# Contiguous DRAM layouts for u, its residual copy, w_mod, the raw parameters and the result, and an earlier place for the tables of the second DFTs

## The chip, the core and the metric

The kernel runs on one core of a Trainium2 chip. The core has five engines that run side by side and wait for each other by semaphores: TensorE (PE, matmuls and their weight loads), VectorE (DVE), ScalarE (ACT), GpSimd (POOL) and SyncE (SP, which here only issues DMAs). Sixteen DMA engines move data between DRAM and the core's memory; DMAs are issued from the queues of SP, POOL and ACT, in program order on each. The metric is the device time of one execution in microseconds (us), as the median of several runs.

## What is computed

One residual block with adaptive layer norm. A state-space convolution (S4) of length 2048 runs over 512 channels, then a spatial-shift mixer and a channel MLP follow. Cut to what matters here:

```python
mod = (_silu(c) @ w_mod).reshape(c.shape[0], 6, 1, -1)
sa, ca, ga, sb, cb, gb = (mod[:, 0], mod[:, 1], mod[:, 2], mod[:, 3], mod[:, 4], mod[:, 5])
h = _layernorm(x, axis=-1) * (1 + ca) + sa
x = x + ga * _A_ref(h, ...)          # A_u is x; S4: K = einsum(C, exp(dt*A*l), dt*B).real,
...                                  # y = irfft(rfft(pad(K)) * rfft(pad(h)))[:L] + h * Dskip
h = _layernorm(x, axis=-1) * (1 + cb) + sb
x = x + gb * _B_ref(h, ...)          # gelu(LN(h) @ w1), shifts by +1, -1, +2, -2, @ w2,
...                                  # then gelu(LN @ w3) @ w4
```

All arrays are float32. `A_u` is (1, 2048, 512) and `w_mod` is (512, 3072).

## The kernel before

The convolution is done as a DFT of length 4096, factored into 64 x 64. The order of all work is written out by hand (`tc.manual_schedule()`): each engine runs its instructions in the order of the program text, and the framework adds the semaphores. The stages are:

- *Preparation* (`body`, up to `pr.close()`): small inputs and the raw parameters `raw` (ar, ai, cr, br, ci, bi) are loaded from SP, and the constants PA, CE, C0, PB, C1 from POOL. `load_mod(0..2)` loads three of the six blocks of `w_mod` into parts of the tile KX, and `load_u(0)`, `load_u(1)` load the first half of u into the two buffers of the pool `up` (tiles named `xu`).
- *Generation*: a loop over 32 chunks `k` (`turns`, `products`, `burst`) makes the convolution kernel K and the first DFT of it in KX. Beside it, by the lists `side[k]`, u is normalised (`u_stats`, `u_norm`) and its first DFT (`u_dft`) is stored to the DRAM scratch VU, 128 KB at a time from SP, out of the tiles `vs`. The other blocks of `w_mod` come by `load_mod(3..5)` into the one buffer of the pool `wml`, and the rest of u by `load_u(2)`, `load_u(3)`. POOL copies w2, w3 and w4 from DRAM to a DRAM scratch here.
- `k_first(0..7)`: matmuls with FK out of KX into the tiles VK, evicted by ACT and DVE.
- *Spectral steps*: a loop `n` over 16 steps (jh, kc). `spectrum_k` makes the second DFT of K with the table T2 (in two tiles named `xu`) and a flipped copy T3 of it that POOL makes (`flip`). `multiply` multiplies with the spectrum of u on DVE (tiles ma, mb, then zc). `back` applies the inverse DFT's first half (Gm), ACT copies the result to the tile z (a pool of two buffers) and POOL issues its store to the scratch ZT, in two DMAs of 64 partitions each. `spectrum_u(n + 1)` makes the second DFT of u out of VU with the table TU, and `load_vu(n + 3)` loads VU for a later step into one of seven buffers `ld`. The residual x, the same array as u, is loaded into X2, which is the memory of KX, by `load_x` in the steps 3, 4, 6 and 8. Between the steps also lie the loads of w1, FI and w2 and the first blocks of the inverse.
- *Inverse, mixer, channel MLP*: the inverse reads ZT, adds to X2, and `chan_out` writes each finished block of 128 rows to the result.

The sequences of 32 partitions: u is taken apart as 4 groups of 32 partitions (`bp`), two of them with the rows of time in reverse order, hence four DMAs per `load_u` and `load_x`, and four per block of the result.

PE's code is a straight line of 14,390 instructions.

Of the kernel before, what the change touches and what calls it, by code (L numbers as in the profile page):

```python
# [7 lines left out]
F32 = mybir.dt.float32  # L8
# [13 lines left out]
UB = (1, 2, 0, 3)  # L22
# [61 lines left out]
def layouts(inp):  # L84
    a = lambda n: np.asarray(inp[n])
    perm = lambda x: np.ascontiguousarray(x.reshape(2, 2, 2, 16, 4, -1).transpose(1, 3, 0, 2, 4, 5).reshape(512, -1))
    m = {"u": a("A_u")[0], "wm": a("w_mod"), "c": np.ascontiguousarray(a("c").reshape(4, 128).T),
         "ld": np.ascontiguousarray(perm(a("A_log_dt")).reshape(4, 128).T),
         "dk": np.ascontiguousarray(a("A_Dskip").reshape(2, 2, 2, 64).transpose(0, 2, 1, 3).reshape(4, 128)),
         "w1": a("B_w1"), "w2": a("B_w2"), "w3": a("B_w3"), "w4": a("B_w4")}  # L90
    for k, n in (("ar", "A_A_re"), ("ai", "A_A_im"), ("br", "A_B_re"), ("bi", "A_B_im"),
                 ("cr", "A_C_re"), ("ci", "A_C_im")):
        m[k] = perm(a(n))
    m.update(shape_constants())
    return m


def dram(t, off, ap):
    return bass.AP(tensor=t.tensor, offset=t.offset + off, ap=ap)


def body(ctx, tc, A):
    nc = tc.nc
    V, S, P, T, Y = nc.vector, nc.scalar, nc.gpsimd, nc.tensor, nc.sync
# [59 lines left out]
    a12 = ExitStack()  # L164
# [2 lines left out]
    Kq = KX.rearrange("p (g h c) -> p h g c", g=64, h=2)  # L167
    X2 = KX.rearrange("p (b d) -> p b d", b=16)
    up = a12.enter_context(pool("up", bufs=2))
    FK = pa12.tile([128, 128], F32, name="FK")  # L170
    sp1 = pa12.tile([128, 1], F32, name="sp1")
    V.memset(sp1, 0.0)
# [27 lines left out]
    wmt = {}  # L200

    def load_mod(n):
        wmt[n] = KX[:, n * 2048:n * 2048 + 2048].rearrange("p (a b) -> p a b", a=4) if n < 3 else \
            wml.tile([128, 4, 512], F32, name="wm")
        Y.dma_start(wmt[n], dram(A["wm"], MODS[n] * 512, [[3072, 128], [128 * 3072, 4], [1, 512]]))


    def mod_parts(n):
# [16 lines left out]

    def load_u(g):
        x = ut[g] = up.tile([128, 4, 512], F32, name="xu")
        for n, bp in enumerate(UB):
            Y.dma_start(x[n * 32:(n + 1) * 32],
                        dram(A["u"], (bp * 16 + g * 4) * 512, [[64 * 512, 32], [1, 2048]]) if bp > 1 else  # L230
                        dram(A["u"], (bp * 16 + 15 - g * 4) * 512, [[64 * 512, 32], [-512, 4], [1, 512]]))

    pe = a1.enter_context(pool("pe", bufs=2))
    PE, KP = {}, {}
# [42 lines left out]
    with tc.manual_schedule():  # L277
        Y.dma_start(ld[:, :4], A["ld"])
        Y.dma_start(cT, A["c"])
        for k in raw:  # L280
            Y.dma_start(raw[k], A[k].rearrange("(t p) n -> p t n", p=128))
        gate = pp.tile([128, 4], F32, name="gate")
        P.tensor_copy(gate[:, 0:1], raw["ai"][:, 0, 0:1])
        for k, t in (("PA", PA.rearrange("p a b c -> p (a b c)")), ("CE", CE), ("C0", C0),
# [113 lines left out]
        V.tensor_tensor(as4(wn), as4(wn), by(dt), op=OP.mult)  # L398
    pr.close()

    wml = a1.enter_context(pool("wml", bufs=1, reuse_waits="tile"))
    wk = a1.enter_context(pool("wk", bufs=2, reuse_waits="tile"))
    wk1 = a1.enter_context(pool("wk1", bufs=1, reuse_waits="tile"))
    uv = a1.enter_context(pool("uv", bufs=2, reuse_waits="tile"))
# [112 lines left out]
    for i in range(16):  # L517
# [5 lines left out]
        if i % 4 == 3 and i < 8:  # L523
            side[at(i) + 2].append(lambda i=i: load_u(i // 4 + 2))

    def add_skip(h, g0, g1):
        V.tensor_add(Kq[:, h, g0:g1, 31], DS[:, h * 64 + g0:h * 64 + g1], Kq[:, h, g0:g1, 31])

    later = []
    with tc.manual_schedule():  # L530
        turns(0, 0)
        turns(0, 1)
        wps = psu.tile([128, 512], F32, name="pu")
        for i in range(4):
            T.transpose(wps[:, i * 128:i * 128 + 128], wn[:, i * 128:i * 128 + 128], ident)
        act(WN, wps)
        ms = [mod_sum(n) for n in range(2)]
        turns(1, 0)
        for f in ms:
            f()  # L540
        turns(1, 1)
        later.append(mod_parts(2))
        late = [lambda: later.append(mod_sum(2))]
        for k in range(33):
            now, later = later, []
            for f in now:
                f()
            if k + 2 < 32:
                turns(k + 2, 0)
                turns(k + 2, 1)  # L550
            while late:
                late.pop()()
            if k < 32:
                fresh = k % 4 == 1 and k < 28
                if fresh:
                    exps(k // 4 + 1, 0, 2)
                e = products(k)
                if k == 31:
                    warm(8)
                    add_skip(0, 0, 64)  # L560
                    add_skip(1, 0, 56)
                burst(k, *e)
                if k == 31:
                    warm(4)
                if fresh:
                    KP[1] = psk.tile([128, 8, 64], F32, name="kp")
                    fill(3)
                    for u in range(2, 5):
                        exps(k // 4 + 1, u, u + 1)
                        if u < 4:  # L570
# [12 lines left out]
        T2 = [up.tile([128, 16, 128], F32, name="xu") for i in range(2)]  # L583
        load_t2 = lambda i: Y.dma_start(T2[i], A["T2"].rearrange("p (a b) -> p a b", a=32)[:, i * 16:i * 16 + 16])
        load_t2(0)
    a1.close()


    a2 = ExitStack()
    v0x = ExitStack()  # L590
    c2 = a2.enter_context(pool("c2"))
    TU = c2.tile([128, 32, 64], F32, name="TU")
    Gm = c2.tile([128, 2, 64], F32, name="Gm")
    FI = c2.tile([128, 32, 2, 32], F32, name="FI")
    VK = [v0x.enter_context(pool("v0", side="right")).tile([128, 64, 2, 64], F32, name="VK0"),
# [111 lines left out]
        q.dma_start(zis[jh, k][:, a:a + n], dram(ZT[jh], (k * 4 + a) * 32768, [[256, 128], [32768, n], [1, 256]]))  # L707

    def load_x(g):
        for bp in range(4):  # L710
            Y.dma_start(X2[bp * 32:(bp + 1) * 32, g * 4:g * 4 + 4],
                        dram(A["u"], (bp * 16 + g * 4) * 512, [[64 * 512, 32], [512, 4], [1, 512]]))

    def inv_half(jh, g, i, pl, name):
        p = pl.tile([128, 2, 256], F32, name=name)
# [242 lines left out]
    def chan_out(g, acc, i, qs):  # L958
        b = 2 * g + i
        o = c2p.tile([128, 512], F32, name="gf")  # L960
        V.tensor_mul(o, acc[i], mods[5])
        V.tensor_add(X2[:, b], X2[:, b], o)
        for bp in range(4):
            qs[bp % len(qs)].dma_start(dram(A["out"], (bp * 16 + b) * 512, [[64 * 512, 32], [1, 512]]),
                                       X2[bp * 32:(bp + 1) * 32, b])

    def chan(g, hl):
        t = g + 3 if 0 < g < 4 else None
# [114 lines left out]

    steps = [(jh, kc) for jh in range(2) for kc in range(8)]
    with tc.manual_schedule():
        tu = A["TU"].rearrange("p (a b) -> p a b", a=32)
        load_vu(*steps[0])
        Y.dma_start(TU[:, :16], tu[:, :16])
        flip(0)
        Y.dma_start(Gm, A["G"].rearrange("p (a b) -> p a b", a=2))  # L1090
        for r in range(8):
# [7 lines left out]
        for n, st in enumerate(steps):  # L1099
            p = spectrum_k(*st)  # L1100
            multiply(*st, us, p)
            if n == 7:
                v0x.close()
                pw2 = ctx.enter_context(pool("pw2", side="right", reuse_waits="tile"))
                pw1 = ctx.enter_context(pool("pw1", side="right", reuse_waits="tile"))
                W2h, W2l, ldw2 = weights(pw2, WD["w2"], 512, 512, "w2", 4)
                W1h, W1l, ldw1 = weights(pw1, A["w1"], 512, 512, "w1", 4)
            if n > 0:
                back(*steps[n - 1])
            if n == 15:  # L1110
# [185 lines left out]
```

## Time and profile before

| what | value |
|---|---|
| runs | 698.31, 698.88, 703.15 us; median 698.88 |
| the profiled execution | 701.46 us, its span 699.7 us |
| busy share of the span | PE 91%, weight loads 72%, DVE 71%, ACT 47%, POOL 18% |
| mean granted TensorE clock | 0.986 |
| data moved | 86.43 MB, mean 124 GB/s |
| preparation | about 0 to 35 us |
| generation | about 35 to 208 us |
| k_first | about 208 to 223 us |
| spectral steps | about 223 to 315 us |
| inverse, mixer, channel MLP | about 315 to 700 us |

The DMAs that the change touches, by their sizes in the profile: raw parameters 6 x 256 KB, w_mod 6 x 1024 KB, u 16 x 256 KB, x 16 x 256 KB, T2 2 x 1024 KB, TU 2 x 512 KB, result 64 x 64 KB.

How to read the lines of the profile: an instruction is named by its engine, its line in the program ("L666"), its operation and its tiles (output <- inputs). "Idle before, releaser" is the time that the engine stood still just ahead of an instruction and what ended that; "issue" stands for idle time for which the profile shows no releaser. A DMA named with SPq, POOLq or ACTq is its issue on that queue, not its transfer. The DMA share is the mean busy share of the 16 DMA engines; it can read a little over 1. The chain of waits follows the work that ended last back from the end, each time to what released it.

### The profile page before, as it was taken

How to read it: one execution, taken by the hardware profiler on the slowest of the kernel's cores; microseconds unless marked ns; L12 is line 12 of the kernel's file. 1: busy time of each engine (PE TensorE's matmuls, PEld its weight loads, DVE VectorE, ACT ScalarE, POOL GpSimd, SP SyncE). 2: the span in 40 equal slices, each digit the busy share in tenths (PEclk: the TensorE clock that was granted, in tenths of full speed). 3: DMA queues.
4: the chain of work that ended last, by engine and by line, in shares of the span. 5: the costliest groups of instructions: out<-in, count | busy, mean ns of one | idle time of the engine just before them, and what ended most of it. 6: DMA issues, size and time to landing. Idle time of an engine off the chain costs nothing.

```text
span 699.7 us, 16980 instructions
## 1 busy us (share of the span) xinstructions
PE 639.1 (91%) x7195; PEld 507.1 (72%) x7195; DVE 497.8 (71%) x795; ACT 331.9 (47%) x505; POOL 125.3 (18%) x236
## 2 busy tenths in 40 slices
PE   1899999999999588885998999999999999999996
PEld 0456655656569456653778889999899989889895
DVE  7899999999987567995986967566554536363522
ACT  3978998889856344650444633124131222213120
POOL 4011122022103335431661101002010000000000
PEclk9999999999999889998999999999999999999999
DMA  8903274745539999987268111020110201011011
GB/s 269 297 9 89 77 214 116 197 104 176 147 88 349 231 277 327 292 288 243 90 192 303 40 31 31 15 72 20 46 31 16 76 1 42 20 34 27 1 31 30
DMA packets 57731, 86.43 MB, mean 124 GB/s; under 512 B 5812, under 2 KB 43704, under 8 KB 56216
## 3 DMA queue, kind: packets, MB, share of 16 engines
q1 hardware_dynamic: 53320, 66.74, 34.0%
q0 software_dynamic: 3440, 17.57, 7.4%
q10 hardware_dynamic: 896, 1.05, 0.6%
q8 instruction: 56, 0.92, 0.5%
q14 instruction: 19, 0.16, 0.1%
HBM read 59.12 MB, written 32.90 MB: 132 GB/s over the span
## 4 chain that ended last, share of the span: by engine, by line
PE 69%; DVE 17%; issue 4%; DMA 4%; ACT 3%; POOL 1%; SPq 0%; ACTq 0%; DVEq 0%; POOLq 0%
PE pm L829 7%; PE pm L827 7%; PE pm L826 7%; PE pa L950 6%; PE pa L942 6%; PE pa L943 6%; PE xx L446 6%; PE pk L666 3%; PE kp L496 3%; PE pz L688 2%; DVE e L464 2%; DVE e L474 2%; PE pk L612 2%; PE ph L881 2%; PE ph L883 2%
## 5 line engine op out<-in xcount | busy, mean ns | idle before, releaser
L110 ACT ACTIVATE gh<-pm 128x512 fp32r<-128x512 f32 (+1 forms) x48 | 26.9, 561 | 200.6 <-PE pm L829 200.6
L826 PE MATMUL pm<-nh,w3h 128*128 128x256 f32 (+1 forms) x352 | 85.8, 279 | 2.1 <-ACT nh L110 2.1
L827 PE MATMUL pm<-nh,w3l 128*128 128x256 f32 (+1 forms) x352 | 85.7, 279 | 0.1
L934 DVE TENSOR_TENSOR gl<-gf,gh 128x512 fp32r<-128x512 f32 (+1 forms) x48 | 30.8, 643 | 68.3 <-ACT gf L110 68.3
L942 PE MATMUL pa<-w4h,gh 128*128 128x512 f32 (+1 forms) x176 | 69.6, 395 | 0.0
L943 PE MATMUL pa<-w4l,gh 128*128 128x512 f32 (+1 forms) x176 | 68.9, 392 | 0.0
L826 PEld LDWEIGHTS pm<-nh,w3h 128*128 128x128 f32 (+1 forms) x352 | 65.3, 185 | 3.8 <-ACT nh L110 2.3
L827 PEld LDWEIGHTS pm<-nh,w3l 128*128 128x128 f32 (+1 forms) x352 | 65.3, 185 | 2.2 <-DVE w3l L744 0.5
L753 POOL TENSOR_TENSOR rs<-mv,eps_t 128x1 f32<-128x1 f32 (+1 forms) x39 | 11.0, 283 | 281.8 <-DVE mv L759 264.7
L829 PE MATMUL pm<-nl,w3h 128*128 128x256 f32 (+1 forms) x352 | 54.8, 277 | 0.0
L950 PE MATMUL pa<-w4h,gl 128*128 128x512 f32 (+1 forms) x176 | 48.1, 390 | 0.8 <-DVE gl L934 0.8
L447 PE MATMUL xx<-MG,ON 64*128 64x512 f32 x160 | 47.1, 390 | 0.0
L446 PE MATMUL xx<-MG,ON 64*128 64x512 f32 x160 | 47.1, 389 | 0.0
L829 PEld LDWEIGHTS pm<-nl,w3h 128*128 128x128 f32 (+1 forms) x352 | 46.6, 185 | 0.2 <-DVE nl L799 0.2
L666 PE MATMUL pk<-VK,xu 64*64 64x128 f32 x768 | 36.8, 274 | 10.7 <-issue 10.7
L886 DVE TENSOR_TENSOR h<-h,ph 128x512 f32<-128x512 f32 x16 | 11.0, 687 | 45.1 <-PE ph L883 45.1
L666 PEld LDWEIGHTS pk<-VK,xu 64*64 64x64 f32 x768 | 32.7, 135 | 14.0 <-issue 13.2
L464 DVE SCALAR_TENSOR_TENSOR e<-tr,p 128x512 f32<-128x512 f32 x64 | 41.1, 682 | 0.4 <-ACT tr L110 0.4
L496 PEld LDWEIGHTS kp<-e,e 128*32 128x32 f32 x2048 | 30.1, 110 | 13.1 <-issue 7.5
L950 PEld LDWEIGHTS pa<-w4h,gl 128*128 128x128 f32 (+1 forms) x176 | 33.0, 188 | 8.3 <-DVE gl L934 1.2
L473 DVE TENSOR_TENSOR e<-tr,p 128x1024 f32<-128x1024 f32 x32 | 39.0, 1218 | 0.0
L474 DVE TENSOR_TENSOR e<-tr,m 128x1024 f32<-128x1024 f32 x32 | 39.0, 1218 | 0.0
(236 smaller groups left out, 1723.1 us busy)
## 6 DMA issues: line engine op xcount, KB each, us to landing
VU<-vs SPq DMA_DIRECT2D x64, 128.0 KB, 3.1
ld<-VU SPq DMA_DIRECT2D x16, 512.0 KB, 12.3
ZT<-z POOLq DMA_DIRECT2D x30, 256.0 KB, 6.8
ld<-ZT SPq DMA_DIRECT2D x12, 512.0 KB
Dw<-in_w POOLq DMA_DIRECT2D x8, 688.0 KB, 5.0
xu<-in_u SPq DMA_DIRECT2D x16, 256.0 KB, 8.2
KX<-in_u SPq DMA_DIRECT2D x16, 256.0 KB, 14.2
GD<-go SPq DMA_DIRECT2D x16, 256.0 KB, 2.3
```

Source lines behind the costliest of these rows:

```text
L446: T.matmul(x[:, :512], la, ma, start=(i == 0), stop=(i == len(ops) - 1))
L447: T.matmul(x[:, 512:], lb, mb, start=(i == 0), stop=(i == len(ops) - 1))
L464: V.scalar_tensor_tensor(e0[:, 1, a], tr[:, 1, 0], 1.0 - 2.0 * a, mg[:, a], op0=OP.mult, op1=OP.mult)
L474: V.tensor_mul(e1.rearrange("p r d q -> p r (d q)"), tr[:, :, 1], m1s[0][:, u % 2:u % 2 + 1].to_broadcast([128, 2, 512]))
L496: T.matmul(kp[32 * j:32 * j + 32, (k % 2) * 4 + g], e1[:, r, d], e0[:, r, :, d * 32:d * 32 + 32], start=(r == 0), stop=(r == 1), skip_grou ...
L666: T.matmul(p[gh][kk * 64:kk * 64 + 64, i, ro], w, VK[jh][rows, ri * 32 + k1].rearrange("p j g -> p (j g)"), start=(ri == 0), stop=(ri == 1 ...
L826: T.matmul(p, wh[:, k, c], hi[k], start=(k == 0), stop=False)
L827: T.matmul(p, wl[:, k, c], hi[k], start=False, stop=False)
L829: T.matmul(p, wh[:, k, c], lo[k], start=False, stop=(k == 3))
L942: T.matmul(acc[i], gh[:m, e, s], W4h[:m, f], start=(f == 0), stop=False)
L943: T.matmul(acc[i], gh[:m, e, s], W4l[:m, f], start=False, stop=False)
L950: T.matmul(acc[i], gl[:m, e, s], W4h[:m, f], start=False, stop=(f == 10))
```

## The change

The host lays five arrays out so that each DMA reads or writes one contiguous run per partition, and the kernel's DMAs become plain: `load_u` and `load_x` are one DMA of 128 partitions each instead of four of 32; u and x are now two DRAM arrays (u with the two groups reversed on the host); w_mod is cut into its six blocks; the raw parameters come in runs of 2 KB per partition instead of 512 bytes. `chan_out` issues one DMA of 128 partitions per block, and for the last two blocks one of 64 partitions from each of SP and ACT. The result's DRAM array has the shape (16, 128, 512), and the host brings it back into order.

The table T2 was loaded in two halves, the first behind the generation loop and the second in step 0, and TU in two halves, ahead of `k_first` and in step 1. Now `load_t2` is called in chunk 24 (into the buffer that the third part of u has left) and in chunk 31 (into that of the fourth part), and `load_tu` in chunk 29, whole, into the buffer of the pool `wml`. That pool is opened earlier, so that it lives on through the spectral steps; TU has no tile of its own any more.

The diff, cut to its core:

```diff
@@ def layouts(inp)
+    tiled = lambda x: np.ascontiguousarray(x.reshape(4, 128, -1).transpose(1, 0, 2).reshape(128, -1))
+    u = a("A_u")[0].reshape(32, 4, 16, 512)
+    um = np.stack([u[:, bp, ::-1] if bp < 2 else u[:, bp] for bp in UB])
+    m = {"u": np.ascontiguousarray(um.reshape(128, 4, 2048).transpose(1, 0, 2)),
+         "x": np.ascontiguousarray(u.reshape(32, 4, 4, 2048).transpose(2, 1, 0, 3).reshape(4, 128, 2048)),
+         "wm": np.ascontiguousarray(a("w_mod").reshape(4, 128, 6, 512).transpose(2, 1, 0, 3).reshape(6, 128, 2048)),
...
-        m[k] = perm(a(n))
+        m[k] = tiled(perm(a(n)))
@@ body
     up = a12.enter_context(pool("up", bufs=2))
+    wml = a12.enter_context(pool("wml"))
...
-        Y.dma_start(wmt[n], dram(A["wm"], MODS[n] * 512, [[3072, 128], [128 * 3072, 4], [1, 512]]))
+        Y.dma_start(wmt[n].rearrange("p a b -> p (a b)"), A["wm"][MODS[n]])
...
         x = ut[g] = up.tile([128, 4, 512], F32, name="xu")
-        for n, bp in enumerate(UB):
-            Y.dma_start(x[n * 32:(n + 1) * 32],
-                        dram(A["u"], (bp * 16 + g * 4) * 512, [[64 * 512, 32], [1, 2048]]) if bp > 1 else
-                        dram(A["u"], (bp * 16 + 15 - g * 4) * 512, [[64 * 512, 32], [-512, 4], [1, 512]]))
+        Y.dma_start(x.rearrange("p a b -> p (a b)"), A["u"][g])
...
-            Y.dma_start(raw[k], A[k].rearrange("(t p) n -> p t n", p=128))
+            Y.dma_start(raw[k].rearrange("p t n -> p (t n)"), A[k])
...
-    wml = a1.enter_context(pool("wml", bufs=1, reuse_waits="tile"))
...
+    T2, TU = [], []
+
+    def load_t2():
+        T2.append(up.tile([128, 16, 128], F32, name="xu"))
+        i = 16 * (len(T2) - 1)
+        Y.dma_start(T2[-1], A["T2"].rearrange("p (a b) -> p a b", a=32)[:, i:i + 16])
+
+    def load_tu():
+        TU.append(wml.tile([128, 32, 64], F32, name="wm"))
+        Y.dma_start(TU[0], A["TU"].rearrange("p (a b) -> p a b", a=32))
+
+    side[24].append(load_t2)
+    side[29].append(load_tu)
+    side[31].append(load_t2)
...
-        T2 = [up.tile([128, 16, 128], F32, name="xu") for i in range(2)]
-        load_t2 = lambda i: Y.dma_start(T2[i], A["T2"].rearrange("p (a b) -> p a b", a=32)[:, i * 16:i * 16 + 16])
-        load_t2(0)
...
-    TU = c2.tile([128, 32, 64], F32, name="TU")
+    TU = TU[0]
...
     def load_x(g):
-        for bp in range(4):
-            Y.dma_start(X2[bp * 32:(bp + 1) * 32, g * 4:g * 4 + 4],
-                        dram(A["u"], (bp * 16 + g * 4) * 512, [[64 * 512, 32], [512, 4], [1, 512]]))
+        Y.dma_start(X2[:, g * 4:g * 4 + 4].rearrange("p b d -> p (b d)"), A["x"][g])
...
-        for bp in range(4):
-            qs[bp % len(qs)].dma_start(dram(A["out"], (bp * 16 + b) * 512, [[64 * 512, 32], [1, 512]]),
-                                       X2[bp * 32:(bp + 1) * 32, b])
+        n = 128 // len(qs)
+        for k, q in enumerate(qs):
+            q.dma_start(A["out"][b, k * n:k * n + n], X2[k * n:k * n + n, b])
...
-        Y.dma_start(TU[:, :16], tu[:, :16])
...
-            if n == 0:
-                load_t2(1)
-            if n == 1:
-                Y.dma_start(TU[:, 16:], tu[:, 16:])
```

The order of instructions on PE, DVE, ACT and POOL stays as it was, except for ACT's result DMAs at the end. On SP it changes in two places that the prediction speaks of. The first runs from the last block of w_mod in the generation to the last VU load ahead of the first x load. VU<-vs are the stores of u's first DFT, xu<-in_T loads half of T2, ld<-VU is a load for `spectrum_u`. Before:

```order
L205 DMA wm<-in_wm 128x4x512
L432 DMA VU<-vs 64x2x256 x20
L584 DMA xu<-in_T 128x2048
L626 DMA ld<-VU 128x4x256
L1088 DMA TU<-in_TU 128x1024
L1090 DMA Gm<-in_G 128x128
L626 DMA ld<-VU 128x4x256 x3
L584 DMA xu<-in_T 128x2048
L626 DMA ld<-VU 128x4x256
L1119 DMA TU<-in_TU 128x1024
L626 DMA ld<-VU 128x4x256 x2
```

The first half of T2 and TU now stand among the VU stores, and the second half of T2 where the first was. After:

```order
L211 DMA wm<-in_wm 128x2048
L434 DMA VU<-vs 64x2x256 x4
L533 DMA xu<-in_T 128x2048
L434 DMA VU<-vs 64x2x256 x12
L537 DMA wm<-in_TU 128x2048
L434 DMA VU<-vs 64x2x256 x4
L533 DMA xu<-in_T 128x2048
L640 DMA ld<-VU 128x4x256
L1100 DMA Gm<-in_G 128x128
L640 DMA ld<-VU 128x4x256 x6
```

Behind the first VU load there are now only VU loads and Gm up to the first x load. The second place, on SP too, is the x loads in the spectral steps (KX<-in_u, later KX<-in_x), with the VU loads between them. Before:

```order
L626 DMA ld<-VU 128x4x256 x2
L711 DMA KX<-in_u 32x2048 x4
L626 DMA ld<-VU 128x4x256
L711 DMA KX<-in_u 32x2048 x4
L626 DMA ld<-VU 128x4x256 x2
```

Each x load was a group of four DMAs of 32 partitions. After:

```order
L640 DMA ld<-VU 128x4x256 x6
L724 DMA KX<-in_x 128x2048
L640 DMA ld<-VU 128x4x256
L724 DMA KX<-in_x 128x2048
L640 DMA ld<-VU 128x4x256 x2
```

The places in the order are the same; each x load is now one DMA of 128 partitions.

More of the change, by code (lines that the diff above doesn't have):

```diff
@@ L86, in layouts @@
     perm = lambda x: np.ascontiguousarray(x.reshape(2, 2, 2, 16, 4, -1).transpose(1, 3, 0, 2, 4, 5).reshape(512, -1))
-    m = {"u": a("A_u")[0], "wm": a("w_mod"), "c": np.ascontiguousarray(a("c").reshape(4, 128).T),
+    tiled = lambda x: np.ascontiguousarray(x.reshape(4, 128, -1).transpose(1, 0, 2).reshape(128, -1))
[3 more added lines that the diff above has]
+         "x": np.ascontiguousarray(u.reshape(32, 4, 4, 2048).transpose(2, 1, 0, 3).reshape(4, 128, 2048)),
+         "wm": np.ascontiguousarray(a("w_mod").reshape(4, 128, 6, 512).transpose(2, 1, 0, 3).reshape(6, 128, 2048)), "c": np.ascontiguousarray(a("c").reshape(4, 128).T),
          "ld": np.ascontiguousarray(perm(a("A_log_dt")).reshape(4, 128).T),
@@ L1085, in body @@
     with tc.manual_schedule():
-        tu = A["TU"].rearrange("p (a b) -> p a b", a=32)
         load_vu(*steps[0])
-        Y.dma_start(TU[:, :16], tu[:, :16])
         flip(0)
@@ L1289 @@
         aps[name] = nc.dram_tensor(f"in_{name}", a.shape, mybir.dt.from_np(a.dtype), kind="ExternalInput").ap()
-    aps["out"] = nc.dram_tensor("out", (2048, 512), F32, kind="ExternalOutput").ap()
+    aps["out"] = nc.dram_tensor("out", (16, 128, 512), F32, kind="ExternalOutput").ap()
     with tile.TileContext(nc) as tc:
@@ L1294 @@
     r = _run(nc, [arrays], core_ids=[0])
-    return r.results[0]["out"].reshape(1, 2048, 512)
+    return np.ascontiguousarray(r.results[0]["out"].reshape(16, 4, 32, 512).transpose(2, 1, 0, 3)).reshape(1, 2048, 512)
```

## The prediction

> **What bounds the kernel now.** I read the page first, then the stretches, the chain of waits and single groups of the stage that the change touches. The slices of the page (17.5 us each) show PE at 90% or more nearly everywhere, except between 210 and 335 us:
>
> ```profile
> PE   1899999999999588885998999999999999999996
> ...
> PEclk9999999999999889998999999999999999999999
> DMA  8903274745539999987268111020110201011011
> GB/s 269 297 9 89 77 214 116 197 104 176 147 88 349 231 277 327 292 288 243 90 192 303 40 31 31 15 72 20 46 31 16 76 1 42 20 34 27 1 31 30
> ```
>
> There the DMA engines are full (digit 9) but move only 231 to 349 GB/s. This is the stage of the 16 spectral steps. The next rows are single DVE instructions: the first multiply of steps 0, 1, 9 and 15 (start, duration, line).
>
> ```profile
> 225.82 0.69 DVE L676 TENSOR_TENSOR ma<-pk,us 128x512 f32<-128x512 f32 x1 [2.11 <-PE pk L666]
> 229.43 0.68 DVE L676 TENSOR_TENSOR ma<-pk,us 128x512 f32<-128x512 f32 x1
> ...
> 277.30 0.69 DVE L676 TENSOR_TENSOR ma<-pk,us 128x512 f32<-128x512 f32 x1 [0.50 <-PE pk L666]
> ...
> 309.22 0.69 DVE L676 TENSOR_TENSOR ma<-pk,us 128x512 f32<-128x512 f32 x1
> ```
>
> Steps 0 and 1 are 3.61 us apart with no gap on DVE, so 3.6 us is the price of an undisturbed step. Nine steps would take 32.4 us; they take 277.30 - 225.82 = 51.5. In the group of these multiplies (223 to 315 us; the last column is idle time before it and what ended it) DVE stands idle for 21.0 us:
>
> ```profile
> L676 DVE TENSOR_TENSOR ma<-pk,us 128x512 f32<-128x512 f32 x32 | 21.9, 683 | 21.0 <-PE pk L666 17.0 <-ACT us L110 3.5 <-issue 0.5
> ```
>
> What holds PE back in it? The chain of waits from 228 to 280 us names no releaser, only "issue" (start, length):
>
> ```profile
> 231.50 1.74 issue
> ...
> 238.03 5.68 issue
> ...
> 251.01 1.17 issue
> ...
> 257.18 2.13 issue
> ...
> 267.07 2.43 issue
> ...
> 275.34 0.34 issue
> ...
> 277.36 0.55 issue
> ```
>
> Together 14.0 us. The instructions between such gaps are counted in the next rows (stretch, length, then busy time and count of PE, weight loads, DVE, ACT, POOL, clock, DMA share, GB/s):
>
> ```profile
> 233.20:238.03 4.83, 4.79 (x127) 4.38 (x127) 2.73 (x5) 1.96 (x6) 0.60 (x3) 1.00 1.13 179
> 243.70:251.01 7.31, 7.30 (x126) 5.43 (x126) 4.87 (x8) 2.87 (x6) 1.14 (x2) 0.76 1.09 273
> 252.10:257.18 5.08, 5.00 (x127) 3.83 (x127) 3.89 (x8) 1.58 (x3) 4.17 (x4) 1.00 1.03 278
> 259.30:267.07 7.77, 7.76 (x126) 5.26 (x127) 4.43 (x8) 5.21 (x10) 3.69 (x5) 0.78 1.07 242
> ```
>
> Always 127 matmuls and 127 weight loads, 254 instructions. The page's instruction queue and PE's own count fit that:
>
> ```profile
> PE 639.1 (91%) x7195; PEld 507.1 (72%) x7195; DVE 497.8 (71%) x795; ACT 331.9 (47%) x505; POOL 125.3 (18%) x236
> ...
> q8 instruction: 56, 0.92, 0.5%
> ```
>
> 2 x 7195 = 14,390 instructions in 56 packets are 257 per packet of 16 KB. I read the gaps as PE waiting for its next block of code, whose packet queues behind data. The clock falls to 0.76 in the stretch after the long gap. The other wait is ACT's: its copy into z waits for the store of z two steps earlier (a pool of two buffers).
>
> ```profile
> ACT z L110 <- DMA ZT<-z: 13.0, 3, 5.3
> ```
>
> Why are the engines full at so low a rate? Stretches again, same columns:
>
> ```profile
> 16.00:24.00 8.00, 5.20 (x13) 3.36 (x12) 7.80 (x8) 7.32 (x9) 0.00 (x0) 1.00 1.06 396
> 26.00:34.00 8.00, 7.00 (x46) 3.85 (x38) 5.28 (x9) 6.97 (x11) 0.00 (x0) 1.00 1.07 228
> ...
> 228.00:240.00 12.00, 7.81 (x172) 6.02 (x164) 8.78 (x15) 5.46 (x11) 3.64 (x5) 1.00 1.08 191
> 288.00:308.00 20.00, 18.80 (x418) 13.60 (x413) 19.22 (x34) 10.76 (x22) 8.18 (x11) 1.00 1.05 368
> ```
>
> 16 to 24 us is mainly w_mod, 128 partitions at a time in 2 KB runs: 396 GB/s. 26 to 34 us is u, 32 partitions at a time, alternately in 2 KB and 8 KB runs: 228. 228 to 240 us holds the 32-partition loads of the residual x (8 KB runs): 191. 288 to 308 us has no such load, but the stores of z, the VU loads and ZT loads: 368. So the number of partitions per transfer makes the rate, not the run length, and the x loads fill the engines just where PE needs code and ACT needs z stored.
>
> **The change part by part.** The sum is made against the profiled execution, 701.46 us (span 699.7); it lies 2.6 us above the median of the runs, 698.88.
>
> *x in four transfers of 128 partitions instead of sixteen of 32, T2 and TU earlier.* x is 4.19 MB (16 x 256 KB): 22 us of full engines at 191 GB/s, 11 at 368 to 396. Of the tables (3.15 MB), T2's first half and TU leave the stage's head; T2's second half goes out where the first went, so 2.1 MB, 5.7 us at 368, leave it. What must move from 207 us until multiply 9 is then 1.05 (T2) + 13 x 0.524 (VU) + 4.19 (x) + 9 x 0.524 (z stores) + 1.05 (w1) + 1.05 (FI) = 18.9 MB, 51 us at 368: ready at 258. DVE's floor is 225.8 + 9 x 3.6 = 258.2. The two floors meet, so neither has slack. The z buffer sets a third bound:
>
> ```profile
> 259.80 1.08 ACT L110 ACTIVATE z<-pz 128x512 f32<-128x512 f32 x2 [5.28 <-DMA ZT<-z]
> ```
> ```profile
> 261.18 1.14 POOL L692 DMA_DIRECT2D ZT<-z  x2 [4.75 <-ACT z L110]
> ```
>
> The time from issue of a z store to its landing (minimum, median, maximum), first for 222 to 250 us, then for 290 to 312:
>
> ```profile
> DMA to landing us min/median/max: 9.6/10.6/13.6
> ```
> ```profile
> DMA to landing us min/median/max: 2.9/5.5/7.2
> ```
>
> Two steps can't be shorter than copy, the first store's issue and the second's landing: 1.08 + 0.57 + 5.5 to 7.2 = 7.2 to 8.9 us, or 3.6 to 4.4 a step; with the landing of now (10.6) it would be 6.1. I take 4.2, nearer the upper end since engines stay about full: multiply 9 at 263.6, -13.7 us. Ends: 3.6 (-19.1) and 4.9, half way from 3.6 to 6.1 (-7.4). In this sum the code waits shrink to what the full but fast stretch shows, under 0.6 each. What is late next is the z store.
>
> [...]
>
> *Steps 9 to 15.* 309.22 - 277.30 = 31.9 us. Of DVE's 21.0 us idle, 2.1 lie before step 0 and 51.5 - 32.4 = 19.1 before step 9, so hardly any is left here: DVE splits w1 and w2 and adds the first inverse blocks between the multiplies. The 10 MB left go in 27 us at 368 GB/s. So 0; ends -1 (small waits) and +3 (the inverse's ZT loads are issued less time ahead of it). Everything behind, to the end, waits for the last z store and moves along whole.
>
> *The tables in the generation's chunks.* Three loads of 1 MB on SP, among the VU stores. The nearest rows are w_mod's loads of that size there, and PE's gaps without a releaser in these chunks:
>
> ```profile
> wm<-in_wm SPq DMA_DIRECT2D x3, 1024.0 KB, 6.0
> ```
> ```profile
> PEld kp L496 <- issue: 7.5, 21, 0.4
> ```
>
> 6 us from issue to landing, no gap over 0.4. On SP each waits only for the last reader of its buffer (sums of w_mod, DFTs of u), a chunk or more back. The VU stores queued behind may come up to 6 us later; their vs buffers are used again some three chunks on, and a chunk lasts 4.3 us there (two bursts of the chain, then three issues of SP):
>
> ```profile
> 196.72 1.03 PE kp L496 x64
> ...
> 201.03 1.03 PE kp L496 x64
> ```
> ```profile
> 207.10 0.54 SPq L584 DMA_DIRECT2D xu<-in_T  x1
> 209.08 0.38 SPq L626 DMA_DIRECT2D ld<-VU  x1
> ...
> 222.07 3.59 SPq L711 DMA_DIRECT2D KX<-in_u  x4
> ```
>
> VU's first load, at 209.08, has a load of T2 ahead of it before and after. It waits for the last VU stores, which TU now precedes; if they land up to 6 us later, k_first covers it, which ends about 222, when the first load of x is let go. I take +0.5, ends 0 and +1.2 (three gaps of 0.4).
>
> *Raw parameters, w_mod, u.* They load faster, but the first 35 us hang on DVE, ACT and PE; one wait for a load is on record there, and it isn't on the chain:
>
> ```profile
> PE xx L249 <- DMA CE<-in_CE: 0.6, 1, 0.6
> ```
>
> 0, ends -0.6 and 0.
>
> *The result.* Within the run the stores are beside PE work. At the end SP and ACT each issue four (two for each half), now two:
>
> ```profile
> L964 ACTq DMA_DIRECT2D out<-KX x4: 375/410/434, 694.5 to 696.2; - x4
> ```
>
> The last issue, 0.41 us, falls away: -0.4, ends -0.4 and 0 (a landing longer by as much).
>
> Sum: -13.7 + 0 + 0.5 + 0 - 0.4 = -13.6, 687.9 us for an execution like the profiled one and 685.3 for the median. Whether the 2.6 us between them are such waits, which would then go too, can't be seen: 686.5.
>
> **The rivals.**
> - *The undisturbed step:* code and stores keep up, 3.6 a step, and the favourable end of every other term: -19.1 - 1 - 0.6 - 0.4 = -21.1, 677.8 to 680.4 (median and profiled execution). For it: steps 0 and 1. Against: 18.9 MB just fit.
> - *PE's gaps stay:* the engines are still full, and each block waits as before. Then 32.4 + 14.0 us instead of 51.5, -5.1: 694 to 696. For it: the DMA share in all four rows is over 1. Against: from 288 to 308 us it is 1.05 too, and PE is busy for 18.8 of 20. [...]
> - *The x loads don't get faster* (their rate is the mixture with z stores, not the partitions): only the tables' 5.7 us are won, 693 to 696. Against: the row of 26 to 34 us, without z stores.
> - *Slower:* the tables hold up code in the last chunks, where PE is the bound. From 14 us of such gaps on the gain is eaten, and with three gaps of 5.68 (17 us) the time is 702 to 705. Against: w_mod's loads, 0.4.
>
> **How the numbers follow.** Forecast (3.8 to 4.9 a step, 681 to 692): 0.58. Undisturbed step: 0.22. Gaps stay: 0.12. x no faster: 0.05. Slower: 0.03. A measurement of this kernel can tell about 1%, 7 us, from no change, so faster is under 692: 0.58 + 0.22 = 0.80; same 0.12 + 0.05 = 0.17; slower 0.03. The range runs from the undisturbed step (677.8) into the gaps' case (694).
>
> **What would show it.** Right: 350 GB/s or more between 222 and 260 us, no gap of PE over 1 us in the steps, z stores landing in 5 to 7 us, multiply 9 near 264, steps 9 to 15 in 32 us, chunks 24 to 31 as long as now. Wrong: gaps of 2 to 5 us after each 254 instructions; ACT waiting more than 13 us for z stores; inverse waiting for ZT by more than 3 us; load 0 of VU landing after k_first.

## The result and the profile after

| | before | after |
|---|---|---|
| median of the runs (range), first comparison | 698.63 us (698.31 to 703.15) | 691.02 us (689.23 to 692.29) |
| ratio, 95% interval | | 0.9874 (0.9828 to 0.992) |
| median (range), the unchanged kernels once more | 700.41 us (697.42 to 702.38) | 689.36 us (688.27 to 689.80) |
| ratio, 95% interval | | 0.9839 (0.9818 to 0.9859) |
| profiled execution (span) | 701.46 us (699.7) | 691.26 us (689.5) |

The change makes the kernel 1.3 to 1.6% faster. The forecast was 686.5 us, 12.4 us under the median of before that it was made against. By the medians the drop is 7.6 us in the first comparison and 11.0 in the second; between the profiled executions -13.6 us was forecast and -10.2 came out.

The busy tenths and rates of the page of after, in the same 40 slices as before:

```profile
PE   1899999999999998977998999999999999999996
...
PEclk9999999999999999998999999999999999999999
DMA  8603264643739997967387010020100201010001
GB/s 299 284 2 79 75 218 105 209 121 85 275 85 317 354 335 258 346 204 226 108 257 240 1 32 32 16 77 15 47 31 17 77 1 62 1 49 13 1 31 31
```

The four slices of PE from 227 to 297 us, which read 5, 8, 8, 8 before, now read 9, 9, 8, 9. Single instructions: the first multiply of steps 0, 9 and 15 (start, duration, line), then the group of all of them between 223 and 315 us with DVE's idle time before them.

```profile
227.31 0.69 DVE L690 TENSOR_TENSOR ma<-pk,us 128x512 f32<-128x512 f32 x1 [2.12 <-PE pk L680]
...
266.79 0.69 DVE L690 TENSOR_TENSOR ma<-pk,us 128x512 f32<-128x512 f32 x1
...
298.37 0.69 DVE L690 TENSOR_TENSOR ma<-pk,us 128x512 f32<-128x512 f32 x1
```
```profile
L690 DVE TENSOR_TENSOR ma<-pk,us 128x512 f32<-128x512 f32 x32 | 21.9, 684 | 8.9 <-ACT us L115 5.9 <-PE pk L680 2.6 <-issue 0.5
```

DVE waits for PE's pk for 2.6 us there, not 17.0. Steps 0 to 9 take 39.48 us, not 51.48. From the waits between 223 and 315 us (waiting instruction <- what it waited for: total, times, longest):

```profile
ACT z L115 <- DMA ZT<-z: 8.7, 3, 4.3
PEld py L731 <- issue: 8.0, 4, 6.9
PE py L731 <- DMA ld<-ZT: 6.5, 1, 6.5
...
PEld pk L731 <- DMA ld<-ZT: 2.4, 1, 2.4
...
PEld pk L650 <- issue: 1.6, 7, 0.3
...
PE pk L731 <- DMA ld<-ZT: 1.5, 1, 1.5
...
PEld pk L680 <- issue: 0.8, 2, 0.4
...
PEld pz L702 <- issue: 0.5, 1, 0.5
```

In the steps PE's gaps without a releaser are at most 0.5 us (before, up to 5.68 in the chain of waits). The long wait in the rows of py comes behind the steps: the inverse waits 6.5 us for a load of ZT. Before, it waits there as long:

```profile
PE py L719 <- DMA ld<-ZT: 6.9, 1, 6.9
```

What is left in the steps is ACT's wait for the z stores, 8.7 us. The stretch in which the x loads used to fill the engines (start:end, length, busy time of PE, weight loads, DVE, ACT, POOL, clock, DMA share, GB/s), and the landing time of the z stores between 222 and 250 us:

```profile
228.00:240.00 12.00, 11.52 (x271) 9.55 (x266) 11.77 (x21) 6.69 (x13) 3.90 (x6) 1.00 0.97 336
```
```profile
DMA to landing us min/median/max: 5.4/6.4/8.9
```

336 GB/s after 191, 6.4 us after 10.6, and PE busy for 11.5 of 12 us after 7.8.

One wait is new. On SP (the queue's own rows: start, time, line) and on ACT, around the generation's end:

```profile
202.97 1.65 SPq L537 DMA_DIRECT2D wm<-in_TU  x1
204.72 2.57 SPq L434 DMA_DIRECT2D VU<-vs  x4
207.39 0.54 SPq L533 DMA_DIRECT2D xu<-in_T  x1
212.65 0.39 SPq L640 DMA_DIRECT2D ld<-VU  x1
```
```profile
212.79 2.56 ACT L115 ACTIVATE VK<-pk 128x512 f32<-128x512 f32 x5 [4.04 <-DMA xu<-in_T]
```

The first VU load goes out at 212.65, not 209.08, and ACT's first copy into VK starts at 212.79, after 4.04 us of idle time. The time from the generation's last DVE instruction (207.90 before, 208.79 after) to the first multiply grows from 17.92 to 18.52 us.

The account between the two profiled executions, by the starts of the same instructions:

| stretch | predicted | measured |
|---|---|---|
| up to the first multiply | +0.5 | 227.31 - 225.82 = +1.5 |
| steps 0 to 9 | -13.7 | 39.48 - 51.48 = -12.0 |
| steps 9 to 15 | 0 | 31.58 - 31.92 = -0.3 |
| step 15 to the last add of the result | 0 | (684.81 - 298.37) - (695.05 - 309.22) = +0.6 |
| from there to the end of the execution | -0.4 | 6.45 - 6.41 = 0.0 |
| sum | -13.6 | -10.2 |

### The profile page after: what moved, and what is told of

Same layout as the page of the kernel before. It is cut to its first block, busy times and chain, and to the rows that moved or that the text cites. A ratio compares the mean times of both kernels' runs of the same rounds, so it can differ in the third digit from the quotient of the medians.

```text
span 689.5 us, 16884 instructions
## 1 busy us (share of the span) xinstructions
PE 642.6 (93%) x7195; PEld 509.2 (74%) x7195; DVE 498.0 (72%) x795; ACT 331.2 (48%) x505; POOL 124.8 (18%) x236
## 3 DMA queue, kind: packets, MB, share of 16 engines
q1 hardware_dynamic: 46712, 66.74, 30.1%
q10 hardware_dynamic: 864, 1.05, 0.5%
## 4 chain that ended last, share of the span: by engine, by line
PE 70%; DVE 6%; DMA 5%; ACT 3%; POOL 2%; issue 1%; ACTq 0%; SPq 0%; DVEq 0%; POOLq 0%
PE pm L841 7%; PE pm L838 7%; PE pm L839 7%; PE xx L448 7%; PE pa L954 6%; PE pa L955 6%; PE pa L962 6%; PE kp L498 3%; DMA ZT<-z 3%; PE ph L893 2%; PE ph L895 2%; PE ph L892 2%; DMA ld<-ZT 2%; PE pu L426 2%; PE pT L803 2%; PE pk L626 2%
## 5 line engine op out<-in xcount | busy, mean ns | idle before, releaser
L449 PE MATMUL xx<-MG,ON 64*128 64x512 f32 x160 | 48.1, 397 | 0.0
L448 PE MATMUL xx<-MG,ON 64*128 64x512 f32 x160 | 48.0, 396 | 0.0
L498 PEld LDWEIGHTS kp<-e,e 128*32 128x32 f32 x2048 | 30.1, 110 | 12.7 <-issue 7.6
L115 ACT ACTIVATE p<-xx 128x1024 f32<-128x1024 f32 (+1 forms) x40 | 37.5, 979 | 2.2 <-PE xx L252 1.0
L115 ACT ACTIVATE tr<-xx 128x1024 f32<-128x1024 f32 x32 | 33.0, 1030 | 9.6 <-PE xx L449 7.9
```

The lines of the kernel that those rows point to most:

```text
L115: return S.activation(out, in_, f, bias=bias, scale=scale)
L448: T.matmul(x[:, :512], la, ma, start=(i == 0), stop=(i == len(ops) - 1))
L449: T.matmul(x[:, 512:], lb, mb, start=(i == 0), stop=(i == len(ops) - 1))
L498: T.matmul(kp[32 * j:32 * j + 32, (k % 2) * 4 + g], e1[:, r, d], e0[:, r, :, d * 32:d * 32 + 32], start=(r == 0), stop=(r == 1), skip_grou ...
```

## The experiments

The same two or three stretches are read in every trace. In this table, "head" is the time from the last DVE instruction of the generation to the first multiply of step 0; "0 to 9" and "9 to 15" are between first multiplies; medians and ratios are over the runs of that comparison, beside before on the same chip. Between chips compare the ratios, not the medians. The stretches come from one execution each, which can lie some us off the median of its kernel (e4_x32: 701.00 us for 697.06; e6_t2: 692.63 for 688.59).

| kernel | head | 0 to 9 | 9 to 15 | median us | ratio to before (95%) |
|---|---|---|---|---|---|
| before | 17.92 | 51.48 | 31.92 | 698.63 | |
| after | 18.52 | 39.48 | 31.58 | 691.02 | 0.9874 (0.9828 to 0.992) |
| after_again | 19.40 | 40.17 | 31.01 | 689.36 | 0.9839 (0.9818 to 0.9859) |
| e1_x | 17.93 | 40.97 | 31.01 | 690.38 | 0.9852 (0.9821 to 0.9883) |
| e2_tables | 18.64 | 48.78 | 31.01 | 697.74 | 0.9955 (0.9932 to 0.9978) |
| e3_rest | 17.94 | 49.24 | 32.34 | 700.08 | 0.999 (0.9967 to 1.0012) |
| e4_x32 | 18.22 | 51.07 | 32.27 | 697.06 | 0.9943 (0.9921 to 0.9965) |
| e4_xpitch | 18.44 | 44.32 | 56.64 | 718.86 | 1.025 (1.0222 to 1.0277) |
| e5_z3 | 18.49 | 37.77 | 31.79 | 688.51 | 0.9835 (0.9811 to 0.986) |
| e5_flips | 19.35 | 47.79 | 37.71 | 706.16 | 1.008 (1.0052 to 1.0109) |
| e6_tu | 17.93 | 37.75 | 31.43 | 687.88 | 0.983 (0.9806 to 0.9854) |
| e6_t2 | 18.94 | 39.99 | 31.01 | 688.59 | 0.9844 (0.9818 to 0.9869) |
| e7_both | 17.91 | 37.48 | 30.78 | 686.59 | 0.9815 (0.9792 to 0.9839) |
| e8_flips_ahead | 18.79 | 40.37 | 30.60 | 690.14 | 0.9851 (0.983 to 0.9872) |

### Which part carries the gain: x alone, the tables alone, the rest alone

e1_x is before with this alone:

```diff
+     "x": np.ascontiguousarray(a("A_u")[0].reshape(32, 4, 4, 2048).transpose(2, 1, 0, 3).reshape(4, 128, 2048)),
-        for bp in range(4):
-            Y.dma_start(X2[bp * 32:(bp + 1) * 32, g * 4:g * 4 + 4],
-                        dram(A["u"], (bp * 16 + g * 4) * 512, [[64 * 512, 32], [512, 4], [1, 512]]))
+        Y.dma_start(X2[:, g * 4:g * 4 + 4].rearrange("p b d -> p (b d)"), A["x"][g])
```

> The kernel before with the x loads alone changed (one load of 128 partitions from a contiguous copy). Theory X (the 32-partition loads fill the transfer engines and hold up code and the z stores): steps 0 to 9 take 38 to 42 us from the first ma of step 0 to that of step 9, not 51.5, and the total falls by 9 to 12 us against a profiled run of before at 701.5, to 688 to 692. Rival T (the second table halves, which before loads in steps 0 and 1, are part of the load): steps 0 to 9 stay above 45 us and less than 6 us is gained.

e2_tables is before with the table loads alone moved (T2's halves and TU into the generation's chunks 24, 29 and 31, TU in w_mod's buffer):

```diff
+    side[24].append(load_t2)
+    side[29].append(load_tu)
+    side[31].append(load_t2)
...
-            if n == 0:
-                load_t2(1)
-            if n == 1:
-                Y.dma_start(TU[:, 16:], tu[:, 16:])
```

> The kernel before with the tables alone loaded earlier. Theory X: steps 0 and 1 may gain up to 1 us, steps 2 to 9 nothing (50 to 52 us for 0 to 9), and the generation's end loses 0.9 to 1.5 us, since the table load stands ahead of the last VU stores: the total is 0 to 1.5 us longer than before. Rival T: steps 0 to 9 fall below 47 us and the total falls by over 3 us.

e3_rest is after with both of these put back, so that only the layouts of u, w_mod, the raw parameters and the result differ from before.

> The kernel after with the x loads and the tables put back as before (u, w_mod, raw parameters and result stay contiguous). Theory X: the time of before within 1 us, steps 0 to 9 at 50 to 53 us, the first multiply within 0.5 us of before's 225.8, the end after the last multiply unchanged within 0.4 us. Rival R (the contiguous u, w_mod and raw loads or the result stores carry part of the gain): over 2 us faster than before.

x alone gives 10.2 us between the medians (700.58 to 690.38), as much as the whole change. Its stretch shows it (columns as above):

```profile
228.00:240.00 12.00, 10.16 (x239) 8.19 (x235) 10.17 (x18) 6.50 (x13) 4.26 (x6) 1.00 1.05 390
```

The engines are as full as before (1.05 for 1.08) but move 390 GB/s, not 191. Since the tables' second halves still go out in its steps, they stay full longer (15.39 MB at 385 GB/s between 222 and 262 us, for 13.99 at 350 in after), and steps 0 to 9 take 40.97 us where after needs 39.48 to 40.17. The tables alone give 2.8 us (697.74), which neither theory X (up to 1.5 us longer) nor rival T (over 3 us and steps under 47) expected; the trace has shorter steps (48.78) and a longer head (18.64). On top of x they give nothing that can be told from zero: the ratios of e1_x and after lie within each other's intervals. The rest gives 0.1% with an interval on both sides of zero. Its first multiply comes at 225.72 us (before 225.82), so the raw, w_mod and u loads were hidden. Before and e3_rest issue the same loads in their steps and yet differ by 2.2 us there in one execution each (51.48 and 49.24), so where the engines are full and slow such a difference in the table says nothing by itself; the medians do.

### What makes the x loads slow: partitions or the order in DRAM

e4_x32 is after with each load cut in four, from the same contiguous copy, 8 KB in a row for each partition:

```diff
-        Y.dma_start(X2[:, g * 4:g * 4 + 4].rearrange("p b d -> p (b d)"), A["x"][g])
+        for n in range(0, 128, 32):
+            Y.dma_start(X2[n:n + 32, g * 4:g * 4 + 4].rearrange("p b d -> p (b d)"), A["x"][g, n:n + 32])
```

> The kernel after with each x load cut into four loads of 32 partitions, from the same contiguous copy (8 KB in a row for each partition, as before and after). If the count of partitions sets the rate: these loads run at 190 to 230 GB/s again, steps 0 to 9 take 48 to 53 us and the total is 8 to 12 us above after (699 to 702). If the 128 KB pitch of the old copy in DRAM set it: the rate stays at 340 to 390 GB/s, steps 0 to 9 take 39 to 41 us and the total is that of after within 1 us.

```profile
228.00:240.00 12.00, 7.81 (x167) 5.93 (x161) 8.58 (x15) 5.25 (x11) 4.39 (x6) 0.99 1.05 190
```

190 GB/s again, and the steps take 51.07 us in the trace. So for loads of 32 partitions the order in DRAM doesn't set the rate (191 GB/s before, 190 here). Each transfer is also a quarter as large here, 256 KB, and that isn't the cause either. The raw parameters are 256 KB each in 128 partitions, and while in after only they are under way, the engines move 389 GB/s:

```profile
3.80:4.80 1.00, 0.00 (x0) 0.00 (x0) 0.83 (x6) 0.00 (x0) 0.00 (x0) 1.00 1.01 389
```

What is left is the count of partitions in a transfer: with x in loads of 32 this stretch reads 190 and 191 GB/s, in loads of 128 336 (after) and 390 (e1_x). What in the hardware makes the difference, no run shows. The median is 697.06 us, under the expected 699 to 702: it is that of e2_tables (697.74), which has the same earlier tables and its 32-partition loads from the old order.

PE's gaps come back too, though nothing of PE's program was changed. From the chain of waits (start, length):

```profile
231.50 1.03 issue
237.32 4.59 issue
...
255.81 2.27 issue
264.24 3.27 issue
```

And the stretches between two such gaps:

```profile
232.53:237.32 4.79, 4.78 (x127) 4.21 (x127) 3.28 (x6) 2.54 (x6) 1.18 (x3) 1.00 1.04 178
258.08:264.24 6.16, 6.16 (x126) 4.36 (x126) 4.82 (x9) 4.36 (x9) 3.33 (x5) 1.00 1.07 248
```

252 to 254 instructions again between gaps. This is what the reading as code packets behind data asks for. The instruction queue q8 moved 4 packets, 0.07 MB, between 222 and 262 us of this trace, and from 228 us on the chain has four gaps over 0.5 us that begin in that stretch. Which packet ended which gap the trace doesn't say.

e4_xpitch asks the converse, 128 partitions from the old order in one load:

```diff
+        Y.dma_start(X2[:, g * 4:g * 4 + 4].rearrange("p b d -> p (b d)"),
+                    dram(A["uo"], g * 2048, [[16 * 512, 4], [64 * 512, 32], [1, 2048]]))
```

> The kernel after with x read from the old order in DRAM, whose rows for neighbouring partitions lie 128 KB apart, in one load of 128 partitions. The four-part loads from the contiguous copy ran at 185 to 215 GB/s, so the count of partitions sets the rate: here it stays at 340 to 400 GB/s, steps 0 to 9 take 38 to 41 us, and the total is that of after within 1 us; a new copy of u was not needed. Rival: the pitch costs something of its own, steps 0 to 9 take over 42 us and the total is over 2 us above after.

It missed by 29 us, to 718.86. The busy tenths and rates of 222 to 262 us in 40 slices, and SP's queue:

```profile
DMA  9997999322329756888999698886232222988999
GB/s 362 334 342 216 152 209 172 85 72 82 82 82 221 234 193 188 225 237 296 311 246 362 167 221 270 250 274 221 94 131 107 98 108 110 253 233 232 364 246 322
```
```profile
238.32 2.81 SPq L640 DMA_DIRECT2D ld<-VU  x1
241.18 13.13 SPq L724 DMA_DIRECT2D KX<-in_uo  x1
```

```profile
ld<-VU SPq DMA_DIRECT2D x5, 512.0 KB, 28.6
```

For microseconds on end the engines are busy to 2 or 3 tenths and move 72 to 85 GB/s, while the VU loads behind land 28.6 us after their issue (the last row: the median of those issued in this stretch). By an estimate from these rows and e1_x's 390 GB/s that is about 4 of 16 engines at close to the rate each has there (82 / 4 = 20 GB/s, against 390 / 16 = 24); 2 to 3 tenths of 16 are 3.2 to 4.8. Why so few, no run shows. Most of the 29 us is lost between multiplies 9 and 10: there the chain of waits stands on the load of w1 that SP issued behind the last x load (start, length):

```profile
261.01 35.94 DMA ld<-in_w
```

The question of the pitch itself this run does not answer, because its load differs from that of after in the form of its DRAM side too, written as 4 x 32 rows and not as 128; it stays open.

### What is late next: the z stores, the flips

e5_z3 is after with a third z buffer. The room comes from T3's third buffer and from Gm, which is loaded into FK's memory once k_first has read it:

```diff
-        t = t3s[kc] = c2.tile([128, 8, 64], F32, name="T3", bufs=3)
+        t = t3s[kc] = c2.tile([128, 8, 64], F32, name="T3", bufs=2)
-        z = s2.tile([128, 4, 256], F32, name="z")
+        z = s2.tile([128, 4, 256], F32, name="z", bufs=3)
+        Gm = FK.rearrange("p (a b) -> p a b", a=2)
+        Y.dma_start(FK, A["G"])
```

> The kernel after with three buffers for z, not two (room from two T3 buffers for three, and Gm loaded into FK's memory after its last use). Theory Z (the z store is what is late next: ACT's eviction of z waits for the store of two steps earlier, 8.7 us in the trace of after): these waits go, a step falls from 4.39 us to 3.7 to 4.0 us, and the total falls by 3.5 to 6 us to 685 to 687.5. Rival C (the step is bound by the chain of PE, DVE and ACT, and the waits are only slack used up): the waits go, the step stays at 4.2 to 4.4 us, under 2 us gained.

ACT's waits for z stores are gone from its trace, all of them. Steps 0 to 9 fall by 1.7 to 2.4 us only (37.77, or 4.20 a step), and by the ratio (0.9835 against 0.9839 and 0.9874) no gain can be told from zero. So removing 8.7 us of waiting won some 2 us: the rival's number was nearer. But the wait was not mere slack, as the rival has it. PE's gaps without a releaser grow in its place (223 to 315 us; in after no such row of PE's matmuls is in that list):

```profile
PE pk L679 <- issue: 2.8, 4, 1.3
...
PE pk L649 <- issue: 0.9, 2, 0.7
```

In the chain of waits from 222 to 270 us the z stores fall from 35.2% to nothing, the time without a releaser grows from 5.0 to 12.0%, and POOL's flips from 7.3 to 13.0%. PE's matmuls wait for flips no longer than in after (1.5 and 1.6 us), so the T3 buffer that was given up costs no such wait.

e5_flips cuts POOL's flip in two, one half in each step:

```diff
-            if n % 2 == 0 and n < 14:
-                flip(steps[n + 2][1])
+            if n < 14:
+                flip(steps[n // 2 * 2 + 2][1], (n % 2,))
```

> The kernel after with the flips on POOL cut in two, half a flip in each step, not a whole one in every second step. If the flips (2 x 1.5 us) hold up the z stores behind them on POOL: the waits of z fall from 8.7 us to under 5 us and 1 to 4 us are gained. If the waits come from the store's own landing time: 0 within 1 us.

It got 15 us slower than after, and for another reason than either theory has. The second half now stands on POOL behind the z store of the odd step, and the next step starts with it:

```profile
PEld pk L682 <- POOL T L664: 19.7, 7, 3.3
PE pk L682 <- POOL T L664: 18.1, 7, 3.0
```

e8_flips_ahead keeps the halves, but makes each two steps earlier (flip(0) and flip(2) ahead of the steps):

```diff
+        flip(2)
...
+            if n < 12:
+                flip(steps[n // 2 * 2 + 4][1], (n % 2,))
```

> The kernel after with half a flip in each step, made two steps further ahead than in the last try (the first two flips before the steps), so that no step waits for its flip. If the flips on POOL hold up the z stores: the waits of ACT's z fall from 8.7 us to under 5 us, and 1 to 3 us are gained. If the z stores' own landing time makes those waits: the waits stay at 7 to 12 us, no change within 1 us. Either way the waits of PE for flips, 18 us in the last try, are gone.

```profile
ACT z L115 <- DMA ZT<-z: 13.0, 3, 4.6
```

The waits for flips are gone, those for z stores stay (13.0 us), and so does the time. The stores land as in after (6.6 us, median of 222 to 250 us, for 6.4). So the store's own landing makes that wait, not the flips.

### The new wait: TU, T2 and the VU stores

ACT's copy into VK waited for 4.04 us, and the trace names T2's load as the releaser. Two kernels tell it apart. e6_tu moves TU one chunk up, e6_t2 moves T2's second half behind the third VU load:

```diff
-    side[29].append(load_tu)
+    side[28].append(load_tu)
```
```diff
-    side[31].append(load_t2)
...
             if r == 6:
                 load_vu(*steps[2])
+                load_t2()
```

> The kernel after with the TU load one chunk of the generation earlier. Theory V (ACT's first VK eviction waits for the last VU stores, which stand behind the TU load): that wait shrinks from 4.0 us and the first multiply comes 0.6 to 1.5 us earlier, the total falls by as much. Rival L (ACT waits for the second T2 load itself, which shares a semaphore with the stores): no change within 0.4 us.

> The kernel after with the second T2 load behind the third VU load, in the first DFT of K. Rival L (ACT's first VK eviction waits for the T2 load): the wait of 4.0 us shrinks by 1.5 us or more and the first multiply comes 0.6 to 1.5 us earlier. Theory V (it waits for the VU stores behind the TU load): the eviction starts within 0.5 us of its time in after, the first VU load is issued where it was, no change within 0.5 us in the total.

e6_tu, SP's queue and ACT's first copy:

```profile
205.95 1.51 SPq L533 DMA_DIRECT2D xu<-in_T  x1
208.94 0.39 SPq L640 DMA_DIRECT2D ld<-VU  x1
```
```profile
209.24 0.60 ACT L115 ACTIVATE VK<-pk 128x512 f32<-128x512 f32 x1 [1.83 <-PE pz L626]
```

e6_t2:

```profile
204.15 2.69 SPq L434 DMA_DIRECT2D VU<-vs  x4
212.63 0.38 SPq L639 DMA_DIRECT2D ld<-VU  x1
...
215.70 0.51 SPq L533 DMA_DIRECT2D xu<-in_T  x1
```
```profile
212.71 2.55 ACT L115 ACTIVATE VK<-pk 128x512 f32<-128x512 f32 x5 [4.46 <-PE pk L625]
```

With T2 out of the way nothing moves: the first VU load at 212.63 and the copy at 212.71, as in after. With TU earlier both are back at 209. The landing times of the last eight VU stores (196 to 216 us) agree, first in after, then in e6_tu:

```profile
DMA to landing us min/median/max: 5.7/6.0/6.4
```
```profile
DMA to landing us min/median/max: 2.4/2.9/3.7
```

So the wait is for the last VU stores, which TU delays, and not for the load that the trace names as releaser. How TU delays them so long stays open: in e6_t2 the DMA share is 0.09 from 210 to 212 us, while SP and ACT still wait. The head is 17.91 to 17.94 us in every kernel without this wait (before, e1_x, e3_rest, e6_tu, e7_both) and 18.22 to 19.40 in the nine with it.

### The kernels together

> The kernel after once more, unchanged, as the measure for the three beside it: 689 to 693 us, steps 0 to 9 in 38 to 41 us, ACT's first VK eviction held up for about 4 us again.

As expected: 689.36 us, the same wait (ACT's first copy into VK at 212.21 us), steps 0 to 9 in 40.17 us.

e7_both takes the third z buffer and the earlier TU:

> The kernel after with three z buffers and the TU load one chunk earlier. If the two gains are separate (the TU load moves the first multiply up by 1.5 to 1.9 us, the buffers take 1.5 to 3 us from the steps): 685 to 687 us, 4 to 6 us under after. If the lower time of the run with the earlier TU load was chance of its steps, or both shorten the same waits: 687 to 688.5 us.

e7_both has the lowest time, 686.59 us: 0.9815 of before, and 2.8 us under after_again in the same comparison. Its five runs reach from 685.91 to 689.90, and the intervals of the two ratios overlap, so the total alone doesn't settle that it beats after. In the traces the first multiply comes 1.5 us earlier than in after_again (225.26 for 226.73), that of step 9 4.2 us (262.74 for 266.90), and the last add of the result 3.1 us (680.03 for 683.17). But in these traces the two cures are not separate. The first multiply of step 9 comes at 266.79 and 266.90 in the two executions of after, at 263.60 with the buffers, at 263.12 with TU, at 262.74 with both. Each alone takes nearly all of it. With TU earlier ACT still waits 10.5 us for z stores in this stretch, and taking that away as well brings 0.4 us.

## Why the prediction held, and where it was off

- **The x loads fill the engines, by their partitions: right.** x alone carries the gain, and cut to 32 partitions from the same contiguous copy it runs at 190 GB/s, not 336, and takes the gain back.
- **PE's gaps are its code behind data: right as far as runs can show it.** In the trace of before q8 has one packet in each of the windows 230 to 231, 240 to 241, 249 to 250, 256 to 257 and 266 to 267 us, within or just before the gaps that begin at 231.50, 238.03, 251.01, 257.18 and 267.07. The gaps fall from 14.0 us in all to at most 0.5 each with faster x loads, and return (4.59, 3.27, 2.27 us, after 252 to 254 instructions) with slow ones. "Always 127" in the prediction is not exact: two of its own rows have 126 matmuls, so its stretches hold 252 to 254 as well. The rival in which they stay is out. But "under 0.6 each" holds for after and not for every kernel with fast x loads: where the engines stay full at 390 GB/s, gaps of up to 1.6 us remain (e1_x), and 1.5 with the third z buffer.
- **4.2 us a step: mis-sized.** The trace has 39.48 / 9 = 4.39, and 4.46 in the second execution: 1.7 to 2.4 us of the 13.7 were not won. The step gave the bound to the z buffer ("What is late next is the z store"). The wait was there, 8.7 us, with a landing time (6.4 us) within the 5.5 to 7.2 that were used, but taking it away wholly gave back some 2 us, and starting the transfers 3.1 to 3.7 us earlier gave as much without touching it. The nearer description in the same part is "The two floors meet, so neither has slack": z, VU, x and the code share the same engines (the page of after gives each queue as a share of 16 engines: q1 30.1%, q0 7.4%, q8, the code's, 0.6%), and with the z wait gone the time without a releaser grows from 5.0 to 12.0% of the chain. That late data costs at the other end is argued, not shown apart. Which of them ends step 9 in e7_both, still 4.16 us a step and not 3.6, was not tried.
- **The tables, +0.5: the cover failed.** The step was "if they land up to 6 us later, k_first covers it". k_first itself waits: ACT's first copy into VK needs the VU stores landed, and SP's first VU load too. That costs 0.6 us of head in the profiled execution and 1.5 in the second. The other 0.9 of the +1.5 is the end of the generation, at 208.79, which lies at 207.33 in the second execution of the same kernel, so nothing shows it to be the change's.
- **The tables' leaving the stage: hidden behind x.** They were 2.1 MB of the sum. Alone they give 2.8 us, on top of x nothing that can be told from zero.
- **Raw parameters, w_mod, u, 0: right** (e3_rest: ratio 0.999, 0.9967 to 1.0012).
- **The result stores, -0.4: nothing.** From the last add to the end of the execution it is 6.41 us before and 6.45 after. It is the other end of the bound given; whether the last transfer, now twice as large, lands later was not measured by itself.
- **Steps 9 to 15, 0: right** (-0.3 and -0.9). Behind step 15, where the account has +0.6, the second execution of after is 0.6 us shorter than before (683.17 - 297.91 = 385.26 for 385.83), so that is scatter of single executions.
- **The signs.** Between 222 and 260 us the rate is 347 GB/s, and 351 in the second execution, for "350 or more". One sign of being wrong did show, the inverse waiting over 3 us for ZT (6.5 us). It stood before as well (6.9 us), so it could not tell.
- **The base.** Half of the 2.6 us between the profiled execution and the median was counted as won as well. In the later comparisons before lies at 700.4 to 700.8, so this can't be told.

## What to carry to other kernels

Where the DMA engines read full at half the rate of another stretch (here 191 GB/s, for 336 to 390), look at the partitions per transfer first: sixteen loads of 32 partitions cost this kernel 10 us, not by being waited for, but through what queued behind them: the z stores (10.6 us to landing, 6.4 after) and, as PE's gaps are read here, code. A wait in the list is not its price: 8.7 us of waiting for z stores were worth some 2 us, because other waits took their place, and only a run without the wait could tell. A load that is moved to a free place has the same queue's stores behind it (here 6.0 us to landing, for 2.9 with TU one chunk earlier), so look for who needs those stores landed.

## What was not expected of the hardware

- A load of 128 partitions whose DRAM side is written as 4 x 32 rows ran at 72 to 85 GB/s with 2 to 3 tenths of the engines busy, and the VU loads in that stretch landed after 28.6 us (median). With x in plain 128 rows they land in 6.2 us.
- The x load in one transfer of 128 partitions lands in 8.0 us (median). Cut into four of 32 partitions, one of the four alone lands in 15.4 us, though the bytes and their order in DRAM are the same.
